# Window attention, forward and backward: y products and the weight gradient group between the two pairs as two 128x64 column tiles each

## The chip, the cores and the metric

The kernel runs on one core of a Trainium2 chip. The time is the device time of one execution, in microseconds. Before the change it is 2059.06 us, the median of five runs (2056.26 to 2065.65).

## The reference

A 256 x 256 image with 384 channels (C) is cut into windows of 8 x 8 tokens. Each window of 64 tokens attends to itself with one head. The kernel must return the output and the gradients for `x`, `wqkv` and `wo`, in bfloat16.

```python
xw = windows(x)                              # (1024, 64, 384)
q, k, v = split(xw @ wqkv)                   # three times 384
p = softmax(einsum('bqc,bkc->bqk', q, k) * C ** -0.5)
o = einsum('bqk,bkc->bqc', p, v) @ wo
out = windows_back(o)
out, vjp = jax.vjp(forward, x, wqkv, wo)
return out, *vjp(grad_out)                   # dx, dwqkv, dwo
```

## The kernel before

The weights are folded in a prologue: A = Wq Wk^T (scaled), B = Wv Wo, and their transposes AT and BT. So per token only four products with 384 x 384 matrices are left: y = x A, z = dO B^T, u = x B and v = x A^T.

Two windows above each other fill the 128 partitions; four such pairs of windows side by side make a "quad", and there are 128 quads. The loop over quads is a software pipeline written out by hand in `step(c, b, a)`. In one pass it works on three quads: `a` gets its products z and y, `b` its scores, softmax, u and v and the first half of its attention products, and `c` (the quad before) the second half. `manual_schedule` keeps the order in which the code issues instructions, on each engine. SP issues the loads of x and all DMA transposes, POOL the loads of the incoming gradient and the stores of both outputs.

TensorE's order in one pass is:

- `scores(b)` (L165): 24 products of 64 columns, full 128x128 tile.
- `uv(b)` (L219): u and v, 24 products of 384 columns, 128x128.
- `project(a, 0, mo)` (L147): z, 9 products of 512 columns, 128x128.
- `filler(1)`: one PSUM tile of the weight gradient, if a group is waiting (L281): 12 products of 384 columns, 128x128. A group is made after every three quads (`GQ = 3`) and has six such tiles, so two fillers a pass keep up with it.
- `attend(c, (2, 3), b)`: for each of two window pairs 8 products in 64x64 tiles (L249), then four products in 128x64 tiles (L264), then `turn(b)` (L227), eight products of 128 columns in 128x64 tiles.
- `project(a, 1, mo)` (L147): y, 9 products of 512 columns, 128x128; then SP's transpose of y and z into `tok`.
- `filler(1)`: a second weight gradient tile, 12 products of 384 columns, 128x128.
- `attend(b, (0, 1))`: as above in 64x64 and 128x64 tiles, without a turn.

All PSUM tiles come in turn from one ring of eight banks. A product waits until the bank's holder of eight allocations earlier has been read. In this order the second window pair's `pd` follows `pg`, the weight gradient tile, by eight allocations, and the three tiles of y (`pj`) follow `pu`, `pw` and `pd` of the pair before. ACT evicts z, y, u, v, `po` and `pd`; DVE evicts `pu`, `pw` and the turned tile, and adds `pg` to the float32 sum `GF_acc` (L283).

A tile's shape follows from its operands: a stationary operand of 64 columns, whose product goes to one half of the 128 PSUM partitions (`LO` or `HI`), takes half of the array's columns. Two such products, one on each half, make a pair.

Of the kernel before, what the change touches and what calls it, by code (L numbers as in the profile page):

```python
# [14 lines left out]
P = 128  # L15
WIN = 8
WT = WIN * WIN
# [5 lines left out]
def kernel(  # L23
# [21 lines left out]
    nc = tc.nc  # L45
    _, H, W, C = x.shape
    CK = C // P
# [39 lines left out]
    for dst, left, lo, right, ro, sc in (  # L87
# [5 lines left out]
        for mr in range(CK):  # L93
            pc = ring.tile([P, C], F32, tag="r")
            for mc in range(CK):
                nc.tensor.matmul(pc[:], lhsT=left[:, lo + mc, mr * P:(mr + 1) * P], rhs=right[:, ro + mc, :],
                                 start=(mc == 0), stop=(mc == CK - 1))
# [11 lines left out]
    LO, HI = slice(0, WT), slice(WT, P)  # L109
    OTHER = {0: HI, WT: LO}  # L110

    def load(st):
        bp, t0 = st["at"]
        st["xq"] = xq = grp.tile([P, QUAD, C], BF16, tag="xq", name="xq", bufs=2 * GQ + 4)
        st["dq"] = dq = qp.tile([P, QUAD, C], BF16, tag="dq", name="dq", bufs=6)
        for t in range(QUAD):
            nc.sync.dma_start(out=xq[:, t, :], in_=dram_tile(x, bp, t0 + t))
            nc.gpsimd.dma_start(out=dq[:, t, :], in_=dram_tile(grad_out, bp, t0 + t))  # L118
# [11 lines left out]
    def grad_turn(st, t):  # L130
# [4 lines left out]
            nc.tensor.transpose(pt[:, m, :], st["dq"][:, t, m * P:(m + 1) * P], ident[:])  # L135
        nc.vector.tensor_copy(out=st["dT"][:, t, :, :], in_=pt[:])

    ENG = {"D": nc.vector.tensor_copy, "A": nc.scalar.copy}

    def project(st, kind, mo):  # L140
        if kind == 0 and mo == 0:
            st["yz"] = qp.tile([P, CK, QUAD, 4, WT], BF16, tag="yz", name="yz")
        yz = st["yz"]
        wgt, src = ((BT_sb, st["dT"]), (A_sb, st["xT"]))[kind]
        pj = ring.tile([P, QUAD, 2, WT], F32, tag="r")
        for m in range(CK):
            nc.tensor.matmul(pj[:].rearrange("p t w k -> p (t w k)"), lhsT=wgt[:, m, mo * P:(mo + 1) * P],  # L147
                             rhs=src[:, :, m, :], start=(m == 0), stop=(m == CK - 1))
        if kind == 0:
            ENG[EV["z"][mo]](out=yz[:, mo, :, 0:4:3, :], in_=pj[:])  # L150
        else:
            ENG[EV["y"][mo]](out=yz[:, mo, :, 1:3, :], in_=pj[:])  # L152

# [5 lines left out]
    def scores(st):  # L159
        yz, xT = st["yz"], st["xT"]  # L160
        st["sd"] = sd = ring.tile([P, QUAD, 2, WT], F32, tag="r", name="sd")
        for t in range(QUAD):
            for w in range(2):
                for m in range(CK):
                    nc.tensor.matmul(sd[:, t, w, :],  # L165
                                     lhsT=yz[:, m, t, 2 * w:2 * w + 2, :].rearrange("p s k -> p (s k)"),
                                     rhs=xT[:, t, m, w * WT:(w + 1) * WT],
                                     start=(m == 0), stop=(m == CK - 1))

    def over_k(ap, n=P):  # L170
        return ap.unsqueeze(2).broadcast_to([n, QUAD, WT])

    def soft(st, step):
        sd = st["sd"]
        if step == 0:
# [36 lines left out]
    def uv(st, t, part):  # L212
        if t == 0 and part == 0:
            for n in ("uq", "vq"):
                st[n] = qp.tile([P, QUAD, C], BF16, tag=n, name=n)
        wgt, dst, cp = ((B_sb, st["uq"], ENG[EV["u"][t]]), (AT_sb, st["vq"], ENG[EV["v"][t]]))[part]
        pj = ring.tile([P, C], F32, tag="r")
        for m in range(CK):
            nc.tensor.matmul(pj[:], lhsT=st["xT"][:, t, m, :], rhs=wgt[:, m, :],  # L219
                             start=(m == 0), stop=(m == CK - 1))  # L220
        cp(out=dst[:, t, :], in_=pj[:])  # L221

    def turn(st):
# [17 lines left out]
    def attend(st, pair, after=None):  # L241
        bp, t0 = st["at"]
        if pair[0] == 0:
            st["Uq"] = grp.tile([P, QUAD, C], BF16, tag="Uq", name="Uq")
            st["Wq"] = grp.tile([P, QUAD, C], BF16, tag="Wq", name="Wq")
        def both(straight, crossed):
            for h, o, (dst, lhs, rhs, done) in ((LO, LO, straight), (LO, HI, crossed), (HI, LO, crossed),
                                                (HI, HI, straight)):
                nc.tensor.matmul(dst[o, :], lhsT=turned(st, lhs, t, h), rhs=st[rhs][h, t, :], start=True, stop=done)  # L249

        made = []
        for t in pair:
            po, pu, pw, pd = [ring.tile([P, C], F32, tag="r", name=n) for n in ("po", "pu", "pw", "pd")]
            both((pu, "ST", "xq", True), (po, "PT", "uq", True))
            osb = ob.tile([P, C], BF16, tag="o")
            ENG[EV["o"][t]](out=osb[:], in_=po[:])  # L256
            ENG[EV["U"][t]](out=st["Uq"][:, t, :], in_=pu[:])  # L257
            both((pw, "Pb", "dq", True), (pd, "ST", "vq", False))
            ENG[EV["W"][t]](out=st["Wq"][:, t, :], in_=pw[:])  # L259
            made.append((t, pd))  # L260
            store(out_0, osb, bp, t0 + t)
        for t, pd in made:
            for w, o in ((0, HI), (1, LO)):
                nc.tensor.matmul(pd[o, :], lhsT=st["ps"][:, w, t, :], rhs=st["tok"][:, :, t, w, :], start=False,  # L264
                                 stop=True)
            dsb = ob.tile([P, C], BF16, tag="d")
            ENG[EV["d"][t]](out=dsb[:], in_=pd[:])  # L267
            store(out_1, dsb, bp, t0 + t)
        if after is not None:
            turn(after)  # L270
# [3 lines left out]
    def gf_group(sts):  # L274
        n = len(sts) * QUAD
        for f in range(2):
            for ma in range(CK):
                pw = ring.tile([P, C], F32, tag="r", name="pg")
                for i in range(n):
                    st, t = sts[i // QUAD], i % QUAD  # L280
                    nc.tensor.matmul(pw[:], lhsT=st["xq"][:, t, ma * P:(ma + 1) * P],  # L281
                                     rhs=st["UW"[f] + "q"][:, t, :], start=(i == 0), stop=(i == n - 1))
                nc.vector.tensor_tensor(out=GF_acc[:, f, ma, :], in0=pw[:], in1=GF_acc[:, f, ma, :], op=ALU.add)  # L283
                yield

    def filler(n):
        while n and fill:
            try:
                next(fill[0])
                n -= 1  # L290
            except StopIteration:
                fill.pop(0)

    def step(c, b, a):


        def on(st):
            return (lambda f, *r: f(st, *r)) if st is not None else (lambda f, *r: None)
        C_, B, A = on(c), on(b), on(a)
        B(scores)  # L300
        B(soft, 0)
        B(uv, 0, 0)
        B(uv, 0, 1)
        B(soft, 1)
        B(uv, 1, 0)
        B(uv, 1, 1)
        B(soft, 2)
        B(soft, 3)
        B(uv, 2, 0)
        B(uv, 2, 1)  # L310
        for t in range(QUAD):
            A(grad_turn, t)
        B(uv, 3, 0)
        B(uv, 3, 1)
        B(soft, 4)
        for mo in range(CK):
            A(project, 0, mo)
        B(soft, 5)
        filler(1)
        if c is not None:  # L320
            attend(c, (2, 3), b)
        else:
            B(turn)
        for mo in range(CK):
            A(project, 1, mo)
        A(to_tokens)
        filler(1)
        B(attend, (0, 1))

    G_ON_PE = 0  # L330
# [3 lines left out]
    n = len(sts)  # L334
    AHEAD = 3
    with tc.manual_schedule(engines=MANUAL):
        for i in range(min(AHEAD, n)):
            load(sts[i])
            if i < AHEAD - 1:
                load_turn(sts[i])  # L340
        held = []
        get = lambda i: sts[i] if 0 <= i < n else None
        for i in range(-1, n + 1):
            if AHEAD <= i + AHEAD < n:
                load(sts[i + AHEAD])
            if AHEAD - 1 <= i + AHEAD - 1 < n:
                load_turn(sts[i + AHEAD - 1])
            step(get(i - 1), get(i), get(i + 1))
            if i > 0:
                held.append(sts[i - 1])  # L350
                sts[i - 1] = None
            if held and (len(held) == GQ or i == n):
                fill.append(gf_group(held))
                held = []
        filler(1 << 30)

    GFb = setup.tile([P, 2, CK, C], BF16, tag="GFb")
# [9 lines left out]
    for ma in range(CK):  # L367
        for i, (lhs, f, rhs, r0) in enumerate(((GFT, 0, w_sb, C), (GFb, 0, w_sb, 0), (GFT, 1, woT_sb, 0))):
            pe = ring.tile([P, C], F32, tag="r")
            for mb in range(CK):  # L370
                nc.tensor.matmul(pe[:], lhsT=lhs[:, f, mb, ma * P:(ma + 1) * P], rhs=rhs[:, mb, r0:r0 + C],
                                 start=(mb == 0), stop=(mb == CK - 1))
# [6 lines left out]
    for mc in range(CK):  # L379
        pe = ring.tile([P, C], F32, tag="r")  # L380
        for ma in range(CK):
            nc.tensor.matmul(pe[:], lhsT=w_sb[:, ma, 2 * C + mc * P:2 * C + (mc + 1) * P], rhs=GFb[:, 1, ma, :],
                             start=(ma == 0), stop=(ma == CK - 1))
# [32 lines left out]
```

## Time and profile before

| | us |
|---|---|
| median of five runs | 2059.06 |
| lowest and highest run | 2056.26, 2065.65 |
| the profiled execution | 2071.71 |
| its span | 2069.9 |
| PE busy (matmuls) | 2040.5 |
| PEld busy (weight loads) | 1110.9 |
| ACT, POOL, DVE busy | 1467.7, 1419.0, 1382.7 |
| granted TensorE clock | 0.997 of full |

Rows of groups read: line, engine, operation, output <- inputs, tile, shape, count, busy time, mean length in ns. The name before `<-` is the tile that is written. "128*64" is the tile of the array, "128x384" the moving operand. PE is the matmul, PEld the weight load. Matmuls overlap in the records: their ends are modelled, and a matmul's recorded length goes beyond the start of the next one. The timeline merges neighbouring instructions of one group into one line with a count; its first column is the start of the first of them.

The groups that the change touches:

| group | count | mean ns |
|---|---|---|
| L147 y: pj <- xT, A_sb, 128x128, 512 columns | 1152 | 380 |
| L281: pg <- Uq or Wq, xq, 128x128, 384 columns | 3072 | 326 |
| L227: turn, 128x64, 128 columns | 1024 | 219 |
| L264: pd <- tok, ps, 128x64, 384 columns | 1024 | 338 |
| L249: four kinds, 64x64, 384 columns | 4096 | 328 to 335 |

### The profile page before, as it was taken

To read this page: it belongs to the slowest core of one execution; us is meant where nothing else is said; L and a number is where in the kernel's file an instruction comes from. 1 tells how busy PE (TensorE), PEld (TensorE's weight loads), DVE (VectorE), ACT (ScalarE), POOL (GpSimd) and SP (SyncE) were. 2 spreads that over 40 slices of the span, in tenths; PEclk is the share of its full clock that TensorE was granted. 3 is DMA by queue.
4 is the path that set the end of the run, shared out by engine and by line. 5 is a ranking of instruction groups with operands and counts; after the bars stand their busy time and mean duration, and the time that the engine had idled before them with its cause. 6 is when DMAs were issued, how large, how long until landed. Compare 5 with 4: busy or idle time off the path is not lost.

```text
span 2069.9 us, 49158 instructions
## 1 busy us (share of the span) xinstructions
PE 2040.5 (99%) x17790; PEld 1110.9 (54%) x17790; DVE 1382.7 (67%) x3107; ACT 1467.7 (71%) x3213; POOL 1419.0 (69%) x2566
## 2 busy tenths in 40 slices
PE   8999999999999999999999999999999999999998
PEld 4454455555555555555555555555555555555554
DVE  5666566666666666666666666666666666666665
ACT  5776677777777777777777777777777777777773
POOL 4665777676776676677777666677777667677764
PEclk9999999999999999999999999999999999999999
DMA  9999999999999999999999999999999999999993
GB/s 204 202 203 179 191 205 200 199 199 200 201 211 192 204 207 198 198 211 203 204 203 200 207 191 211 194 206 205 199 204 205 202 200 204 202 204 193 207 178 77
DMA packets 997172, 408.92 MB, mean 198 GB/s; under 512 B 880704, under 2 KB 971584, under 8 KB 996928
## 3 DMA queue, kind: packets, MB, share of 16 engines
q1 hardware_dynamic: 873648, 253.80, 73.0%
q0 software_dynamic: 122880, 151.68, 31.9%
q8 instruction: 139, 2.28, 0.5%
q14 instruction: 105, 0.86, 0.1%
q10 hardware_dynamic: 400, 0.29, 0.0%
HBM read 101.84 MB, written 101.84 MB: 98 GB/s over the span
## 4 chain that ended last, share of the span: by engine, by line
PE 92%; DMA 4%; ACT 1%; POOL 1%; issue 1%; DVE 1%; POOLq 0%; ACTq 0%; SPq 0%
PE pj L147 23%; PE pg L281 23%; PE pj L219 22%; PE pd L264 5%; PE pu L249 5%; PE sd L165 5%; PE pw L249 4%; PE pd L249 3%; DMA out_dram<-dsb 2%; PE pt L227 1%; DMA out_dram<-osb 1%; POOL out_dram L239 1%; DMA tok<-yz 1%; DMA dq<-in_grad_out_dram 1%; ACT uq L221 0%
## 5 line engine op out<-in xcount | busy, mean ns | idle before, releaser
L239 POOL DMA_DIRECT2D out_dram<-osb x1024 | 576.6, 570 | 348.9 <-ACT osb L256 214.7
L239 POOL DMA_DIRECT2D out_dram<-dsb x1024 | 571.4, 563 | 226.5 <-DMA dq<-in_grad_out_dram 69.7
L283 DVE TENSOR_TENSOR GF_acc<-pg,GF_acc 128x384 f32<-128x384 f32 x258 | 143.8, 557 | 474.7 <-PE pg L281 474.7
L281 PEld LDWEIGHTS <-xq 128*128 128x128 bf16 x3072 | 300.1, 98 | 227.0 <-DVE pr L202 2.2
L219 PEld LDWEIGHTS <-xT 128*128 128x128 bf16 x3072 | 292.9, 98 | 190.7 <-issue 10.1
L256 ACT CAST osb<-po 128x384 bf16<-128x384 f32 x512 | 221.9, 484 | 239.4 <-PE pu L249 139.8
L219 PE MATMUL pj<-AT_sb,xT 128*128 128x384 bf16 x1536 | 335.3, 328 | 5.6 <-ACT dsb L267 4.1
L219 PE MATMUL pj<-B_sb,xT 128*128 128x384 bf16 x1536 | 335.3, 328 | 0.0
L118 POOL DMA_DIRECT2D dq<-in_grad_out_dram x512 | 274.0, 550 | 54.8 <-DMA out_dram<-osb 16.8
L221 ACT CAST uq<-pj 128x384 bf16<-128x384 f32 x512 | 247.5, 483 | 73.0 <-PE pj L219 68.8
L257 DVE CAST Uq<-pu 128x384 bf16<-128x384 f32 x512 | 280.6, 548 | 7.4 <-PE pu L249 7.3
L259 DVE CAST Wq<-pw 128x384 bf16<-128x384 f32 x512 | 280.6, 548 | 0.0
L281 PE MATMUL pg<-Uq,xq 128*128 128x384 bf16 x1536 | 270.4, 326 | 0.9 <-DVE pr L202 0.7
L147 PE MATMUL pj<-xT,A_sb 128*128 128x512 bf16 x1152 | 271.0, 380 | 0.0
L147 PE MATMUL pj<-dT,BT_sb 128*128 128x512 bf16 x1152 | 270.0, 379 | 0.2 <-DMA dT<-dq 0.2
L281 PE MATMUL pg<-Wq,xq 128*128 128x384 bf16 x1536 | 270.0, 326 | 0.0
L267 ACT CAST dsb<-pd 128x384 bf16<-128x384 f32 x512 | 222.0, 483 | 54.1 <-DMA out_dram<-dsb 17.5
L152 ACT CAST yz<-pj 128x512 bf16<-128x512 f32 x384 | 224.1, 586 | 42.2 <-PE pj L147 26.7
L221 ACT CAST vq<-pj 128x384 bf16<-128x384 f32 x512 | 250.4, 489 | 2.8 <-PE pj L219 0.5
L249 PE MATMUL pw<-dq,Pb 64*64 64x384 bf16 x1024 | 226.1, 329 | 1.1
L249 PEld LDWEIGHTS <-PS 64*64 64x64 bf16 x3072 | 120.3, 105 | 166.3 <-issue 153.4
L198 ACT COPY ps<-Pb 64x256 bf16<-64x256 bf16 x256 | 103.1, 403 | 149.6 <-DVE Pb L195 148.1
(61 smaller groups left out, 2366.9 us busy)
## 6 DMA issues: line engine op xcount, KB each, us to landing
xq<-in_x_dram SPq DMA_DIRECT2D x512, 96.0 KB, 4.2
dq<-in_grad_out_dram POOLq DMA_DIRECT2D x512, 96.0 KB, 5.4
out_dram<-osb POOLq DMA_DIRECT2D x1024, 48.0 KB, 4.5
out_dram<-dsb POOLq DMA_DIRECT2D x1024, 48.0 KB, 4.4
dT<-dq SPq DMA_TRANSPOSE x128, 5.9
xT<-xq SPq DMA_TRANSPOSE x128, 7.5
tok<-yz SPq DMA_TRANSPOSE x128, 8.5
w_sb<-in_wqkv_dram SPq DMA_DIRECT2D x1, 864.0 KB, 6.2
```

The costliest lines, as they stand in the source:

```text
L118: nc.gpsimd.dma_start(out=dq[:, t, :], in_=dram_tile(grad_out, bp, t0 + t))
L147: nc.tensor.matmul(pj[:].rearrange("p t w k -> p (t w k)"), lhsT=wgt[:, m, mo * P:(mo + 1) * P], rhs=src[:, :, m, :], start=(m == 0), stop ...
L152: ENG[EV["y"][mo]](out=yz[:, mo, :, 1:3, :], in_=pj[:])
L219: nc.tensor.matmul(pj[:], lhsT=st["xT"][:, t, m, :], rhs=wgt[:, m, :], start=(m == 0), stop=(m == CK - 1))
L221: cp(out=dst[:, t, :], in_=pj[:])
L239: nc.gpsimd.dma_start(out=dram_tile(dst, bp, t)[WIN * w:WIN * (w + 1)], in_=src[h, :])
L249: nc.tensor.matmul(dst[o, :], lhsT=turned(st, lhs, t, h), rhs=st[rhs][h, t, :], start=True, stop=done)
L256: ENG[EV["o"][t]](out=osb[:], in_=po[:])
L257: ENG[EV["U"][t]](out=st["Uq"][:, t, :], in_=pu[:])
L259: ENG[EV["W"][t]](out=st["Wq"][:, t, :], in_=pw[:])
L267: ENG[EV["d"][t]](out=dsb[:], in_=pd[:])
L281: nc.tensor.matmul(pw[:], lhsT=st["xq"][:, t, ma * P:(ma + 1) * P], rhs=st["UW"[f] + "q"][:, t, :], start=(i == 0), stop=(i == n - 1))
```

## The change

A helper `product` issues either one matmul or two. With `split[0]` set it takes each half of the stationary operand's 128 columns and writes the matching half of the output's partitions. The moving operand is the same for both. `split[0]` is set in `step` between the attention products of the pairs (2, 3) and those of (0, 1), so it covers y and the second filler. Outside it, and for z, the scores, u, v and the first filler, one 128x128 matmul is issued as before. Nothing else is moved.

```diff
+    ALL = False
+    split = [ALL]
+
+    def product(out, lhsT, rhs, start, stop):
+        if split[0]:
+            for h in (LO, HI):
+                nc.tensor.matmul(out[h], lhsT=lhsT[:, h], rhs=rhs, start=start, stop=stop)
+        else:
+            nc.tensor.matmul(out, lhsT=lhsT, rhs=rhs, start=start, stop=stop)
...
         for m in range(CK):
-            nc.tensor.matmul(pj[:].rearrange("p t w k -> p (t w k)"), lhsT=wgt[:, m, mo * P:(mo + 1) * P],
-                             rhs=src[:, :, m, :], start=(m == 0), stop=(m == CK - 1))
+            product(pj[:].rearrange("p t w k -> p (t w k)"), wgt[:, m, mo * P:(mo + 1) * P], src[:, :, m, :],
+                    m == 0, m == CK - 1)
...
-                    nc.tensor.matmul(pw[:], lhsT=st["xq"][:, t, ma * P:(ma + 1) * P],
-                                     rhs=st["UW"[f] + "q"][:, t, :], start=(i == 0), stop=(i == n - 1))
+                    product(pw[:], st["xq"][:, t, ma * P:(ma + 1) * P], st["UW"[f] + "q"][:, t, :], i == 0, i == n - 1)
...
             attend(c, (2, 3), b)
         else:
             B(turn)
+        split[0] = True
         for mo in range(CK):
             A(project, 1, mo)
         A(to_tokens)
         filler(1)
+        split[0] = ALL
         B(attend, (0, 1))
```

The products of `scores` and `uv` are also written with `product`; they run where `split[0]` is off.

More of the change, by code (lines that the diff above doesn't have):

```diff
@@ L164, in scores @@
                 for m in range(CK):
[L165 to L168, printed above, removed]
+                    product(sd[:, t, w, :], yz[:, m, t, 2 * w:2 * w + 2, :].rearrange("p s k -> p (s k)"),
+                            xT[:, t, m, w * WT:(w + 1) * WT], m == 0, m == CK - 1)
     def over_k(ap, n=P):
@@ L218, in uv @@
         for m in range(CK):
-            nc.tensor.matmul(pj[:], lhsT=st["xT"][:, t, m, :], rhs=wgt[:, m, :],
-                             start=(m == 0), stop=(m == CK - 1))
+            product(pj[:], st["xT"][:, t, m, :], wgt[:, m, :], m == 0, m == CK - 1)
         cp(out=dst[:, t, :], in_=pj[:])
@@ L354 @@
                 held = []
+        split[0] = False
         filler(1 << 30)
```

## The prediction

> **What bounds the kernel now.** I read the page from its busy rows down, then the chain of waits, then TensorE's timeline through one steady quad.
>
> ```profile
> PE 2040.5 (99%) x17790; PEld 1110.9 (54%) x17790; DVE 1382.7 (67%) x3107; ACT 1467.7 (71%) x3213; POOL 1419.0 (69%) x2566
> PEclk9999999999999999999999999999999999999999
> DMA  9999999999999999999999999999999999999993
> PE 92%; DMA 4%; ACT 1%; POOL 1%; issue 1%; DVE 1%; POOLq 0%; ACTq 0%; SPq 0%
> ```
>
> TensorE carries the chain, at full clock. "99% busy" hides something, though: a matmul's recorded length (326 ns for 384 columns) is longer than the step to the next one (0.16 us), so a hole of 0.1 or 0.2 us in the issue doesn't show as idle time. Holes have to be read from start to start. This is TensorE's timeline through one quad's middle, with the reduction on DVE and SP's queue below it. The columns are start, length, then what ran. Single pairs are taken from narrower windows of the same timeline.
>
> ```profile
> 1009.28 2.10 PE L147 MATMUL pj<-dT,BT_sb 128*128 128x512 bf16 x9
> 1011.23 2.11 PE L281 MATMUL pg<-Uq,xq 128*128 128x384 bf16 x12
> 1013.27 0.35 PE L249 MATMUL pu<-xq,PS 64*64 64x384 bf16 x1
> ...
> 1013.78 0.32 PE L249 MATMUL pw<-dq,Pb 64*64 64x384 bf16 x1
> 1013.99 0.35 PE L249 MATMUL pd<-vq,PS 64*64 64x384 bf16 x2
> 1014.27 0.52 PE L264 MATMUL pd<-tok,ps 128*64 128x384 bf16 x4
> 1014.46 0.33 PE L264 MATMUL pd<-tok,ps 128*64 128x384 bf16 x2
> 1014.62 0.39 PE L227 MATMUL pt<-ident,ps 128*64 128x128 bf16 x8
> 1014.73 0.28 PE L227 MATMUL pt<-ident,ps 128*64 128x128 bf16 x4
> 1014.79 0.22 PE L227 MATMUL pt<-ident,ps 128*64 128x128 bf16 x2
> 1014.94 2.12 PE L147 MATMUL pj<-xT,A_sb 128*128 128x512 bf16 x9
> 1016.90 2.11 PE L281 MATMUL pg<-Wq,xq 128*128 128x384 bf16 x12
> 1018.94 0.35 PE L249 MATMUL pu<-xq,PS 64*64 64x384 bf16 x1
> ...
> 1013.38 0.56 DVE L283 TENSOR_TENSOR GF_acc<-pg,GF_acc 128x384 f32<-128x384 f32 x1 [1.11 <-PE pg L281]
> ...
> 1014.46 0.39 PEld L227 LDWEIGHTS <-ps 128*64 128x64 bf16 x8
> ...
> 1017.71 4.17 SPq L156 DMA_TRANSPOSE tok<-yz  x1
> ```
>
> Steady steps: nine 512-column products take 1.95 us (1009.28 to 1011.23), 0.216 us each. Twelve 384-column products step by 0.1625 us. From about 240 us to the end of the loop every quad takes 15.717 us within a few ns (the start times of the trace, kept to the nanosecond), and TensorE's list of waits is empty for 240 to 2020 us. Only the first dozen quads are longer, by 8.9 us together.
>
> Holes: each change of tile shape has one. Within the turn (L227) the pairs start at 1014.62, .68, .73, .79, so 0.056 us apart, but the first y product follows the last pair by 0.15 us (152 ns in the median of 127 places). The second y product then comes after 226 ns instead of 216. A second kind of hole is a wait: of the last group of four 64x64 tiles, pw starts at 1013.78, its partner pd only at 1013.99, 0.05 us after DVE's sum of pg ends (1013.38 + 0.56 = 1013.94). pd gets the PSUM buffer that pg held eight allocations earlier.
>
> **The change part by part.**
>
> *The shape change between turn and y goes.* Turn already runs as 128x64, and y now does too. The first y pair should follow the last turn pair by 56 ns instead of 152: 96 saved. The slow first step goes too: 10 more. That is 0.106 us a quad. The y buffers allow it: y0's buffer is released by a DVE cast (Uq) 543 ns before y0 starts today, y1's 737 and y2's 1059 ns ahead, constant in every steady quad. Against 106 ns that leaves 0.4 us at least.
>
> *9 products of 512 and 12 of 384 columns become pairs.* The trace holds the very form: L264 and L227 are pairs of 128x64 tiles on the two halves of one PSUM bank, L227 with the same moving operand (ident) for both tiles. The two of a pair start 3.5 ns apart. L264's second pair to the next pair is 0.16 us (1014.46 to 1014.62), as for one 128x128 product of 384 columns (0.1625). L227's 128-column pairs step by 56 ns. Columns per ns come out alike (384/162.5 = 2.36, 512/216 = 2.37), so the columns streamed set the step, and the two halves stream together. I take 0 ns per pair. Bounds: not below zero, since a pair can't stream faster than its columns; above, 25 ns, which is what the first pair after a change of shape takes more (1014.27 to 1014.46 is 0.187 to the ns, against 0.1625), because its successor's weights were not loaded ahead. There are some 1150 y pairs and (3072 - 84)/12/2 = about 125 pg tiles with 12 pairs, 1500: 2650 in all. The upper bound would be 2650 x 25 ns = 66 us. I take zero because L227's loads and pairs are the same case, in steady state.
>
> *Here a rule speaks against the change.* The row is L227's PEld row: eight loads in 0.39 us, beginning at 1014.46 while L264's last pair was streaming, and four pairs then run at 56 ns. The Trainium skill, "TensorE: Matmul & The Clock Gate", Part 3 (What overlaps and what doesn't), says that a weight load runs beside matmuls in flight only when its row group differs. Both column tiles span all rows, so by that rule each pair would expose its loads: at 0.11 us (the recorded load) 2650 pairs cost 290 us, and the kernel would be near 2335. By the row, two loads and two matmuls fit in 56 ns, against 162 or 216 available, so the loads cost nothing. I follow the row. What the row cannot show is a run of twelve 384-column pairs or any 512-column pair, which is why the range keeps some of this.
>
> *The next change of shape moves from 128x128-to-64x64 to 128x64-to-64x64.* The trace has no such step. Neighbours: 128x128 to 64x64 takes 256 - 162.5 = 93 ns, 64x64 to 128x64 takes 276 - 159 = 117, 128x64 to 128x128 96. So between -93 (no drain at all) and about +24. I cost it at nothing either way, since the wait of pd for the sum of pg covers it: pd starts 975 ns after the last pg product whatever the four groups between do, and 203 ns of that is slack. Without the cover, +24 ns x 124 would be 3 us. The cover moves with pg and stays; the second half of the last pg pair starts 3.5 ns later, so pd does too. This takes 0.0035 us a quad back.
>
> *More instructions.* 2650 more matmuls and as many loads, no new DMA, no new instruction on DVE, ACT, POOL or SP. Scores (L165) issue a load and a matmul every 29 ns, so four in 162 ns are no limit. Each eviction waits for the later half: the 3.5 ns again. No wait is added, but SP's transpose of tok waits for y's last eviction (1017.71); it comes 0.1 us earlier in the quad. ACT's y evictions and POOL's stores keep their order.
>
> Sum: 0.106 - 0.0035 = 0.1025, say 0.10 to 0.11 us a quad; x 127 = 13.5 us. In the first dozen quads, where other waits last longer, part of it is swallowed: 0 to 1.3 us. I take 13 us. Against the profiled execution (span 2069.9, its own time 2071.7) that gives about 2058.7. This run lies 12.6 us above the median of the runs shown, so I subtract the same 13 us from the median: 2059.06 - 13 = 2046.
>
> **The rivals.**
>
> *Pairs are not free (slower).* If the loads of a pair can't run ahead when 384 or 512 columns stream, every pair pays part of the load. It decides at 13.5 us / 2650 = 5 ns a pair: above that the change loses. At the 25 ns of an unprepared pair: 66 - 13 = +53, about 2112. If the halves ran one after the other, 1150 x 0.216 + 1500 x 0.1625 = 492 us more. For it: the quoted rule, and that long runs of pairs are nowhere in the trace. Against it: L264's second step, L227's steps, and the 64x64 groups, where four tiles start within 10 ns and step 0.163 us. Chance 0.08.
>
> *Nothing comes of it (same).* The DMA row reads 9 throughout; if transfers kept the quad at 15.7 us, TensorE would meet a wait where the hole was: 2057 to 2059. For it: the DMA row, and the early quads, which do wait for transfers. Against it: quads equal to a few ns for 1800 us, which is no transfer's habit; SP's queue idles before tok's transpose, until y is evicted; dT is issued at 1009.92 and lands 5.9 us later (median), while its first use is some 9 us after that. Also in here: pairs that cost 3 to 5 ns each, 8 to 13 us, eat most of the gain. Chance 0.08.
>
> **How the numbers follow.** The forecast case has 0.84: faster, 2046, its own range 2041 to 2051 (1 us from the sum, and about 4 us for the early quads' luck, which moves the five runs shown between 2056 and 2066). A measurement of this kernel tells about 0.3%, 6 us, from no change, so "same" is 2053 to 2065. The range reaches from 2040 to 2055, taking in pairs of up to 3.5 ns (9 us). Left out are the slower rival and half of the same one. Faster 0.84, same 0.08, slower 0.08.
>
> **What the profile after would show.** Right: y pairs follow the last turn pair by about 0.06 us; nine y pairs take 1.94 us and twelve pg pairs 1.95; from the last pg pair to pd of the second window it is still 0.975 us, whatever the shape change in between takes; the quad takes 15.61 us; no new waits of TensorE after 240 us. Wrong: y or pg pairs step by more than 0.221 or 0.168 us; PEld shows loads only after the preceding pair; a shape change to 64x64 above 0.3 us, so that the wait of pd is no longer what ends last.

## The result and the profile after

The changed kernel takes 2051.25 us (median of 44 runs, 2040.87 to 2072.23). The kernel before took 2063.36 us beside it (79 runs, 2053.46 to 2070.22). The ratio is 0.9946 with a 95% interval of 0.9935 to 0.9957, from runs that nothing disturbed: about 11 us, or 0.5%, faster. The forecast was 2046 us, 13 us less than the 2059.06 us known then, with a range of 2040 to 2055.

These lines of the page after answer to those of before: busy rows, granted clock, DMA, and the chain by engine.

```profile
PE 2024.7 (99%) x20442; PEld 1147.5 (56%) x20442; DVE 1383.7 (67%) x3107; ACT 1465.8 (71%) x3213; POOL 1422.6 (69%) x2566
PEclk9999999999999999999999999999999999999999
DMA  9999999999999999999999999999999999999992
PE 87%; DMA 5%; ACT 2%; issue 1%; POOL 1%; DVE 1%; ACTq 0%; POOLq 0%
```

TensorE issues 2652 matmuls more (the prediction counted 2650), and is busy for 16 us less: a hole in the issue counts as busy here, so closed holes show in this number. They are found in the timeline of one quad (start, length, what ran). First the kernel before: the scores that begin one quad and the next, the products ahead of them, and the loads of y's first weights.

```profile
1004.67 0.87 PE L165 MATMUL sd<-xT,yz 128*128 128x64 bf16 x24
...
1014.94 0.33 PEld L147 LDWEIGHTS <-A_sb 128*128 128x128 bf16 x3
...
1019.94 0.52 PE L264 MATMUL pd<-tok,ps 128*64 128x384 bf16 x4
1020.39 0.87 PE L165 MATMUL sd<-xT,yz 128*128 128x64 bf16 x24
```

Then the changed kernel (helper lines have moved: `product` is L144 for pairs and L146 otherwise), with DVE's sum of pg and the weight loads below.

```profile
1009.28 0.87 PE L146 MATMUL sd<-xT,yz 128*128 128x64 bf16 x24
...
1018.87 0.52 PE L271 MATMUL pd<-tok,ps 128*64 128x384 bf16 x4
1019.22 0.39 PE L234 MATMUL pt<-ident,ps 128*64 128x128 bf16 x8
1019.39 0.22 PE L234 MATMUL pt<-ident,ps 128*64 128x128 bf16 x2
1019.45 2.11 PE L144 MATMUL pj<-xT,A_sb 128*64 128x512 bf16 x18
1021.39 2.12 PE L144 MATMUL pg<-Wq,xq 128*64 128x384 bf16 x24
1023.18 0.33 PE L144 MATMUL pg<-Wq,xq 128*64 128x384 bf16 x2
1023.43 0.35 PE L256 MATMUL pu<-xq,PS 64*64 64x384 bf16 x1
...
1024.16 0.35 PE L256 MATMUL pd<-vq,PS 64*64 64x384 bf16 x2
1024.44 0.52 PE L271 MATMUL pd<-tok,ps 128*64 128x384 bf16 x4
1024.89 0.87 PE L146 MATMUL sd<-xT,yz 128*128 128x64 bf16 x24
1023.55 0.56 DVE L289 TENSOR_TENSOR GF_acc<-pg,GF_acc 128x384 f32<-128x384 f32 x1 [2.56 <-PE pg L144]
1019.39 0.82 PEld L144 LDWEIGHTS <-A_sb 128*64 128x64 bf16 x10
```

From the later matmul of the last turn pair to the first y product it is now 52 ns, where it was 152 (start times of the trace, in ns). Nine y pairs take 1.94 us (1019.45 to 1021.39). The loads of y's first weights start at 1019.39, with the last turn pair; before, they started at 1014.94, with y itself. pd still follows the end of DVE's sum (1023.55 + 0.56 = 1024.11) by 0.05 us. A quad without stalls takes 15.617 us instead of 15.717.

One sign that the prediction named did not hold in this execution: from 240 to 2000 us TensorE has 7 us of waits, 3.9 of them for ACT's eviction of `pd`. Before there were none.

In what follows "quad" is the time from one quad's first score to the next one's, the median in the profiled execution (where more than half of the quads are long, the most frequent value). "Surplus" is what quads from the sixth on take beyond that.

### The profile page after: what moved, and what is told of

Read it like the earlier page. It is cut to its first block, busy times and chain, and to the rows that moved or that the text cites. A ratio compares the mean times of both kernels' runs of the same rounds, so it can differ in the third digit from the quotient of the medians.

```text
span 2052.3 us, 54462 instructions
## 1 busy us (share of the span) xinstructions
PE 2024.7 (99%) x20442; PEld 1147.5 (56%) x20442; DVE 1383.7 (67%) x3107; ACT 1465.8 (71%) x3213; POOL 1422.6 (69%) x2566
## 4 chain that ended last, share of the span: by engine, by line
PE 87%; DMA 5%; ACT 2%; issue 1%; POOL 1%; DVE 1%; ACTq 0%; POOLq 0%
PE pj L146 32%; PE pg L146 11%; PE pg L144 11%; PE pj L144 11%; PE pd L271 5%; PE pu L256 5%; PE sd L146 4%; PE pw L256 4%; PE pd L256 3%; DMA out_dram<-osb 2%; DMA dq<-in_grad_out_dram 2%; DMA out_dram<-dsb 2%; PE pt L234 1%; POOL out_dram L246 1%; ACT uq L228 0%
## 5 line engine op out<-in xcount | busy, mean ns | idle before, releaser
L146 PEld LDWEIGHTS <-xT 128*128 128x128 bf16 x3072 | 291.8, 98 | 186.8 <-issue 4.7
L146 PE MATMUL pj<-AT_sb,xT 128*128 128x384 bf16 x1536 | 333.3, 326 | 3.9 <-ACT dsb L274 3.9
L146 PE MATMUL pj<-B_sb,xT 128*128 128x384 bf16 x1536 | 333.4, 326 | 0.0
L274 ACT CAST dsb<-pd 128x384 bf16<-128x384 f32 x512 | 223.6, 483 | 67.8 <-DMA out_dram<-dsb 28.5
L146 PE MATMUL pj<-dT,BT_sb 128*128 128x512 bf16 x1152 | 269.5, 379 | 2.1 <-DMA dT<-dq 2.1
L144 PE MATMUL pj<-xT,A_sb 128*64 128x512 bf16 x2304 | 270.5, 379 | 0.5 <-ACT osb L263 0.4
L162 ACT CAST yz<-pj 128x512 bf16<-128x512 f32 x384 | 222.9, 589 | 28.4 <-PE pj L144 0.2
L146 PEld LDWEIGHTS <-xq 128*128 128x128 bf16 x1572 | 153.2, 98 | 118.2 <-DVE pr L210 4.5
L144 PEld LDWEIGHTS <-xq 128*64 128x64 bf16 x3000 | 171.1, 110 | 85.6
L160 ACT CAST yz<-pj 128x512 bf16<-128x512 f32 x384 | 206.1, 640 | 0.4 <-PE pj L146 0.2
```

The source lines that it names most:

```text
L144: nc.tensor.matmul(out[h], lhsT=lhsT[:, h], rhs=rhs, start=start, stop=stop)
L146: nc.tensor.matmul(out, lhsT=lhsT, rhs=rhs, start=start, stop=stop)
```

## The experiments

**The changed kernel once more.** No edit.

> The changed kernel once more, to stand beside the others on the same chip. Theory: a steady quad of 15.617 us against 15.717, so about 12.7 us over 127 quads, ratio 0.994. Rival (part of the gain is luck of the first dozen quads, which are bound by transfers): the steady quad is again 15.617, but the ratio of the times wanders by several us with the early stretch.

Measured: quad 15.617 us, surplus 0; median 2046.77, ratio 0.9929 (0.9901 to 0.9957). The earlier profile of the same kernel had a surplus of 13.3 us in nine quads. TensorE has no wait from 240 to 2000 us here. So the quad is firm, and between these two executions, 11.6 us apart, it is the surplus that differs. The lowest runs, 2053.46 before and 2040.87 after, differ by 12.6 us, which is 127 x 0.099 us.

**Only y as pairs.**

```diff
         A(to_tokens)
+        split[0] = ALL
         filler(1)
-        split[0] = ALL
```

> Only y runs as pairs; the gradient group after it is 128x128 again. Theory (what counts is the shape change in the open, pairs are free): the hole between turn and y goes (0.106 us a quad) and one of the same size comes between y and the group (about 0.16 + 0.10 us from last y to first pg, 0.01 more on the first step): the quad stays at 15.71 to 15.72, ratio 1.000. Rival (the pairs of y are faster in themselves, by better weight loads): the quad falls by some part of 0.1 us although the number of shape changes is the same, ratio 0.995 to 0.998.

```profile
714.25 0.39 PE L234 MATMUL pt<-ident,ps 128*64 128x128 bf16 x8
714.47 2.11 PE L144 MATMUL pj<-xT,A_sb 128*64 128x512 bf16 x18
716.51 2.12 PE L146 MATMUL pg<-Wq,xq 128*128 128x384 bf16 x12
718.57 0.35 PE L256 MATMUL pu<-xq,PS 64*64 64x384 bf16 x1
```

Turn to y takes 0.22 us instead of 0.32, but y to pg takes 2.04 instead of 1.95, and the group 2.06 instead of 2.04: the hole has moved behind y. The quad is 15.717 us, exactly that of before. So y's pairs bring nothing in themselves. The time disagrees with "1.000": ratio 0.9973 (0.9957 to 0.9988), median 2055.73. Its profile has no surplus, that of before 14.6 us. Its fastest run, 2053.8 us, is level with the fastest of before, 2053.46. Why this kernel meets fewer long quads at the same quad length was not settled.

**Only the group as pairs.**

```diff
-        split[0] = True
         for mo in range(CK):
             A(project, 1, mo)
         A(to_tokens)
+        split[0] = True
         filler(1)
```

> Only the gradient group after y runs as pairs; y is 128x128 again. Theory: the hole between turn and y stays, a new one of about 0.10 to 0.13 us comes between y and the group, and the change to 64x64 that follows was under the wait for the sum of pg already: the quad gets longer by about 0.12 us, 125 x 0.12 = 15 us, ratio 1.007. Rival (the gain comes from the group's pairs): quad below 15.717, ratio under 1.

```profile
720.96 0.39 PE L234 MATMUL pt<-ident,ps 128*64 128x128 bf16 x8
721.28 2.12 PE L146 MATMUL pj<-xT,A_sb 128*128 128x512 bf16 x9
723.32 2.14 PE L144 MATMUL pg<-Wq,xq 128*64 128x384 bf16 x24
725.39 0.35 PE L256 MATMUL pu<-xq,PS 64*64 64x384 bf16 x1
```

Quad 15.842 us: 0.125 longer than before, 0.12 expected. Both holes are there now: 0.32 from turn to y and 2.04 over y. The group's first pair is slow as well (2.07 over the group). Median 2071.07, ratio 1.0043 (1.0028 to 1.0058), less than the quad alone would make it (127 x 0.125 us, 1.008), again against runs of before that can have surplus (this profile has 1.1 us). Against y only, whose profile has none, it is 15.3 us longer, close to the 15.9 of 127 x 0.125. What counts is how many changes of shape lie in the open, not how many products are pairs.

**Everything but the attention products as pairs.**

```diff
-    ALL = False
+    ALL = True
```

> Every product of scores, u, v, z, y and both groups runs as pairs, so the only shapes left are 128x64 and 64x64. Theory 1 (two loads and two matmuls of a pair fit in about 29 ns, as one load and one matmul of 64 columns do today): the hole between L271 and the scores goes as well, another 0.106 us, the quad falls to about 15.51, ratio 0.987. Theory 2 (loads of 64 columns[...] take about 53 to 56 ns a pair, which the pairs of 128 columns and more hide): u, v, z and the groups stay at their steps, but the 24 score pairs step by 53 to 56 instead of 29 ns, +0.6 us a quad; the quad goes to about 16.1, ratio 1.024. By the rule that loads cannot run beside matmuls of the same rows: every pair pays 0.1 us, over 1.1.

```profile
722.82 0.52 PE L271 MATMUL pd<-tok,ps 128*64 128x384 bf16 x4
723.17 0.92 PE L144 MATMUL sd<-xT,yz 128*64 128x64 bf16 x48
723.93 0.66 PE L144 MATMUL pj<-B_sb,xT 128*64 128x384 bf16 x6
```

24 score pairs take 0.76 us (723.17 to 723.93), 31.5 ns each, against 29.5 for single 128x128 products. Theory 2, with 53 to 56 ns, falls: two loads and two matmuls fit in 32 ns. So does the ratio over 1.1 by the rule quoted in the prediction. The hole before the scores is gone too (0.35 us from L271 to the scores; in the rows above 0.45, before the change and after it). The quad is 15.579 us, less gain than theory 1 had, mostly for the 2 ns on each of 24 pairs. But the kernel is slower: 2076.9 us, ratio 1.0078 (1.005 to 1.0105). There is a surplus of 37 us in 21 long quads, over the first 110 quads, and ACT waits 75.7 us for earlier stores of `dsb` to land. The rows give total, number and longest, from 90 to 2030 us: first the kernel before, then this one.

```profile
ACT dsb L267 <- DMA out_dram<-dsb: 17.5, 13, 4.4
ACT dsb L274 <- DMA out_dram<-dsb: 75.7, 74, 5.9
```

With four output buffers this wait and the surplus are small or large together: 0.2 and 0 us in the second execution of the changed kernel, 17.5 and 15 before, 28.5 and 13 in the first execution of the changed kernel, 75.7 and 37 here.

The remaining runs follow this second bound, and pd's wait.

**pd's wait taken away: column parts in one bank, on both kernels.** The weight gradient tile is made in columns 0 to 255 and then 256 to 383, each with its own sum on DVE.

```diff
-                for i in range(n):
+                for cs in (slice(0, 256), slice(256, C)):
+                    for i in range(n):
...
+                    nc.vector.tensor_tensor(out=GF_acc[:, f, ma, cs], in0=pw[:, cs], ...)
```

> The kernel before, with each weight gradient tile made in two column parts (256, then 128 of its 384 columns), so that the sum on DVE that pd waits for is short at the end (about 0.29 us instead of 0.56). Theory (pd's wait for that sum is what ends last after each group): the hole of about 0.2 us before the last 64x64 products goes, in both groups of a quad, less 0.03 us that the twelve extra products take; quad 15.717 - 0.34 = 15.37 to 15.40, ratio about 0.98. Rival (the hole has another cause, such as weight loads): the hole stays and the quad grows by 0.06 us, ratio 1.004. Stalls by stores may eat some of a gain.

> The changed kernel, with the same two column parts. With the cover gone, the shape change from 128x64 to 64x64 lies in the open. Theory (it costs the same 93 ns as from 128x128): about 0.10 us a quad below the same edit on the kernel before, as with the cover. Rival (the cover hid a dearer change): the difference between the two is under 0.09 us a quad.

On the kernel before:

```profile
717.83 0.83 PE L282 MATMUL pg<-Wq,xq 128*128 128x128 bf16 x12 [0.52 <-DVE GF_acc L284]
...
719.10 0.32 PE L249 MATMUL pw<-dq,Pb 64*64 64x384 bf16 x1
719.10 0.33 PE L249 MATMUL pd<-vq,PS 64*64 64x384 bf16 x2
```

pw and pd start together: the hole before pd is gone, and the attention products take 774 ns instead of 1002. But the second part waits for the sum of the first, since both lie in one tile. The group grows by 0.7 us, and both kernels are slower: 1.0575 (1.0553 to 1.0597) and 1.0529 (1.0507 to 1.055). Their quads, 16.672 and 16.604 us, differ by 0.068, below the 0.09 that spoke for the rival. The waiting group, though, takes 43 ns more as pairs than as single products (2.792 against 2.749 us), which it does neither with one sum (2.047 against 2.043) nor in the next two runs (2.077 against 2.073). So this pair can't judge the cover. Neither has surplus (0.1 us).

**The parts in two banks, on both kernels.**

```diff
-                pw = ring.tile([P, C], F32, tag="r", name="pg")
                 for cs in (slice(0, 256), slice(256, C)):
+                    pw = ring.tile([P, cs.stop - cs.start], F32, tag="r", name="pg")
```

> The kernel before with the two column parts of a weight gradient tile in two PSUM banks, so that the second part need not wait for DVE's sum of the first. Theory (pd's wait for the sum was the cause of the hole; the parts' own wait ate it in the earlier attempt): the eight pairs of attention products take 0.77 us as there, a gain of 0.23 us twice a quad; the group takes 24 products: 12 x (0.109 + 0.056) = 1.98 us plus at most 0.05; quad about 15.717 - 2 x 0.19 = 15.33 if nothing else binds, ratio 0.976. Rival (transfers bind near 15.6, as eight output buffers and all pairs hinted): many quads above 15.4, time 2035 to 2065, with waits for stores, tok or dT.

> The same on the changed kernel. Theory: 0.100 us a quad less than the same edit on the kernel before in quads without stalls (15.23), so the change is worth the same without the cover; ratio 0.970 if nothing else binds. Rival: transfers bind, and the time is no lower than that of the same edit on the kernel before.

Quads without stalls: 15.321 us on the kernel before, 15.215 on the changed one. The difference is 0.106 us with the cover gone, against 0.100 with it: a change from 128x64 to 64x64 is no dearer than one from 128x128. The groups and the first 64x64 product after them, on the kernel before and on the changed one:

```profile
736.44 2.14 PE L282 MATMUL pg<-Uq,xq 128*128 128x256 bf16 x24
738.51 0.35 PE L249 MATMUL pu<-xq,PS 64*64 64x384 bf16 x1
```

```profile
732.06 2.15 PE L144 MATMUL pg<-Wq,xq 128*64 128x256 bf16 x48
734.14 0.35 PE L256 MATMUL pu<-xq,PS 64*64 64x384 bf16 x1
```

With one sum the start times show the same: 256 ns from the last pg matmul to the first 64x64 one, before the change and after it.

Yet the times are 2056.35 us (ratio 0.9974, 0.9935 to 1.0013) and 2090.23 (1.0102, 1.004 to 1.0164). Surplus: 47 us in 33 quads, and 101 us in 72. The order with the shorter quad is the slower kernel. In it ACT, TensorE and POOL waited for (from 90 us on):

```profile
ACT dsb L274 <- DMA out_dram<-dsb: 174.7, 156, 3.7
PE pj L146 <- ACT dsb L274: 17.2, 19, 2.9
POOL out_dram L246 <- DMA dq<-in_grad_out_dram: 149.2, 92, 4.3
```

ACT can't evict `pd`, because an output buffer's last store hasn't landed. The PSUM bank stays taken, and TensorE's products for `pj`, which need the next banks, stand. The kernel before with two banks fits too: 93.7 us of this wait, 47 of surplus.

**Eight, and three, output buffers.**

```diff
-    ob = ctx.enter_context(tc.tile_pool(name="ob", bufs=4))
+    ob = ctx.enter_context(tc.tile_pool(name="ob", bufs=8))
...
```

The run with three has `bufs=3`.

> The changed kernel with eight instead of four buffers for each of the two output tiles (room made by letting two tiles of the epilogue reuse others' space). Theory (the long quads outside steady state come from ACT waiting for stores to land before it can reuse an output buffer, and PSUM banks then held): the steady quad stays 15.617, the long quads after the first five go, the time lies at the lower end of the changed kernel's runs, 2040 to 2044, with little spread. Rival (stores are late because their queue is, and more buffers only delay the wait): same spread and median as the changed kernel, 2045 to 2052.

> Both edits on the changed kernel: column parts and eight output buffers. Theory: quad of about 15.27 to 15.30, no long quads after the first five; 2041 - 127 x 0.33 = about 2000, ratio 0.97. Rival (transfers or stores bind below some quad length): the quad's mean stays above 15.4, with waits of ACT for stores throughout, ratio 0.98 to 1.0.

> The changed kernel with three instead of four buffers for each output tile. Theory (four buffers are enough in the steady quad, and fewer only bring ACT's waits earlier): the steady quad is longer or long quads become more, 2055 to 2100. Rival (few output buffers hold the stores back and leave the transposes room, as eight buffers made tok and dT late): fewer long quads, 2041 to 2046.

With eight: 2084.59 us, ratio 1.0094 (1.0062 to 1.0125), the quad 15.617 but a surplus of 41 us in 47 quads. My theory falls. The waits have moved from the output buffers to what TensorE reads:

```profile
PE pd L271 <- DMA tok<-yz: 20.3, 19, 3.1
PE pj L146 <- DMA dT<-dq: 10.2, 16, 1.3
```

With three: 2107.19 us, ratio 1.0202 (1.0161 to 1.0242), surplus 56 us. So four is better than either. That the four buffers hold the stores back to the good of the transposes would fit the run with eight, but is only argued. With the column parts in one bank the quad is 16.604 us, and there is no surplus with eight buffers or with four (1.0529 both times).

**A quarter of the stores left out**, on the changed kernel with two banks.

```diff
-            store(out_1, dsb, bp, t0 + t)
+            if t % 2 == 0:
+                store(out_1, dsb, bp, t0 + t)
```

> The changed kernel with the column parts in two PSUM banks, and only every second window pair's gradient for x is stored (the other half of out_1 is left out: a quarter of all store traffic and of POOL's store instructions). TensorE, ACT and DVE do the same work. Theory (a quad of 15.215 us is shorter than what the stores' path can follow, and the long quads come from there): the long quads outside the first five go or nearly go, 127 x 15.215 us plus what the changed kernel has beside its quads (2041 - 127 x 15.617 = 58): about 1990 us, ratio 0.965. Rival (the long quads come from the transposes or from TensorE's own order of banks): they stay, 2060 us or more.

Measured: 1992.51 us, about 1990 expected; ratio 0.9669 (0.9633 to 0.9705). The quad is 15.215 and the surplus 0.0 us. POOL now waits for ACT, and ACT for one transfer only (from 90 us on):

```profile
POOL out_dram L246 <- ACT osb L263: 680.0, 240, 6.5
...
ACT osb L263 <- DMA dq<-in_grad_out_dram: 1.7, 1, 1.7
```

So the long quads come from the stores. Whether POOL's issue binds, the engines that carry the packets, or the output buffers, this run doesn't tell apart. It relieves all three, as a buffer that isn't stored is free at once, and the transposes land sooner too (tok 7.6 us after its issue in the median, 10.1 with all stores). That eight buffers didn't help speaks against the buffers alone. No kernel with the full output beat the changed one.

## Why the prediction was right, point by point

*The hole at the shape change.* Right: 0.1025 us a quad forecast, 0.100 measured. By parts, from turn to y it is 100 ns less, not 96: the 152 ns were counted from the later matmul of the last pair and the 56 from the first of a pair; from the later one it is 52. The 10 ns of y's first step went as forecast. Given back are 10 ns, not 3.5: from the last pg pair to pd it is 985 ns, not 975. Of these, 3.5 are the start of the pair's second half; the rest is that DVE's sum starts 371 ns after the last pg matmul instead of 363, for a reason that stays open. y only and group only show that the hole moves with the place of the change: 15.717 and 15.842.

*Pairs cost nothing.* Right for y and pg. The rule on row groups, weighed there against L227's rows, doesn't hold in this kernel: in the all-pairs kernel even the shortest pairs, 64 columns, step by 31.5 ns with two loads each, 2 ns more than one 128x128 product with its load.

*The next shape change lies under pd's wait.* Right in outcome, and needless: it costs the same from either shape, and the two-bank pair gives 0.106 us without the cover.

*The shape change as a rule.* The Trainium skill, "TensorEngine Tiling (Array Packing)", Key Properties, says that changing the mode drains TensorE, and another tile of one mode doesn't. The rows fit that: 152 against 52 ns from turn to y, 258 against 159 from L271 to the scores. They show the cost of a change, not that it is a drain.

*The sum.* 12.7 us from the quads (127 x 0.100), 13 forecast. The measured ratio makes 11 us (9 to 13). That 2051.25 us lies 5 above the forecast is mostly the starting point: 2059.06 was the median of five runs, and 79 runs have 2063.36. From there 13 us less is 2050.4.

*The rival "nothing comes of it".* I argued from quads that agree to a few ns that transfers don't bind. In most quads of 15.6 to 15.7 us they don't, but I took it for a wide margin, and it is a thin one. At 15.617 one of two executions had 13.3 us of surplus, and at 15.579 all pairs had 37. The DMA share was no help: over 300 to 1900 us it is 1.08 before, 1.12 with two banks on the changed kernel, 1.03 with a quarter of the stores gone.

*The early quads.* I counted 0 to 1.3 us swallowed there. The surplus was 14.6 us in the profile of before, 13.3 and 0 in two of after. (The prediction's 8.9 us for the first dozen quads is the sum with the first five, which are 5.7 us shorter than steady ones.) In the first profile of after it doesn't lie in the first dozen quads, but reaches to the 34th. It comes and goes by as much as the change brings.

## What to carry to other kernels

Read TensorE from start to start: a change of tile shape costs about 0.1 us here that no idle column shows. Giving neighbouring products the same shape, as column pairs, removes it, at no price for products of 384 and 512 columns and 2 ns a pair at 64. Count the changes that are left: where one only moves to the next border, as with y only, nothing is won. Before shortening a stage further, test what carries the data away: leaving out part of the stores showed in one run that the next 0.4 us a quad could not be had on TensorE alone.

## What the runs showed of the hardware that was not expected

A stall can be dearer than its length. In the profile of before, TensorE stood 3.77 us for a store, and then ran at half clock. The timeline:

```profile
218.27 1.12 PE L219 MATMUL pj<-AT_sb,xT 128*128 128x384 bf16 x3 [3.77 <-ACT dsb L267]
219.18 1.16 PE L219 MATMUL pj<-B_sb,xT 128*128 128x384 bf16 x3
220.14 1.16 PE L219 MATMUL pj<-AT_sb,xT 128*128 128x384 bf16 x3
```

The same kernel by stretches: length, TensorE's busy time, granted clock, DMA share and GB/s.

```profile
218.20:223.00 4.80, 4.73 (x15) 0.50 0.99 211
223.00:225.00 2.00, 2.00 (x9) 0.78 0.91 191
```

Three products take 0.96 us (219.18 to 220.14) instead of 0.49. The clock is half up to 223 us and, by its mean of 0.78, for 0.9 us of the next two, so for 5.6 us after the stall. Half of that, 2.8 us, is lost on top of the 3.8, and the page's clock row of nines doesn't show it.

From 100 to 2000 us all the traces together have 17 holes of about 2 us and more (1.99 to 3.77) between TensorE's recorded products. Inside 13 of them, or within 1.5 us after, a stretch at half clock began; a hole of 3.48 us with three output buffers had none. The long quads are not explained by it: two banks on the changed kernel, with 101 us of surplus, had one such stretch, of 3.4 us.
